# Six-layer cross network on one core: product 4 at two levels in both tiles, and more places for weights and blocks

## The chip, the cores and the metric

The kernel runs on one core of one Trainium2 chip. The time is device microseconds of the whole program, as the median of its runs. A profiled execution of its own gives the page and the trace.

## The reference

`x0` is [16384, 1024], `ws` is [6, 1024, 1024], `bs` is [6, 1024], all in bf16.

```python
x = x0
for l in range(6):
    proj = jnp.einsum('bd,de->be', x, ws[l]) + bs[l]
    x = x0 * proj + x
return x
```

Each layer is a product of the state x with a square matrix, a bias, an elementwise product with x0 and the addition of the state.

## The kernel before

**Tiles and units.** The 16384 rows are cut into 16 tiles ("pairs" in the code) of 1024 rows, and two tiles make a group that shares the weights of a layer. The work goes group by group, in it layer by layer, in it first tile ("lane 0"), second tile ("lane 1"). One tile in one layer is a *unit*: 96 units. Tiles lie transposed in SBUF, features on the partitions. Three x0 tiles (`x0T0` to `x0T2`, x0) and three state tiles (`xst0` to `xst2`, the running x) are used in turn, tile number modulo 3. So in each group one x0 tile and one state tile are idle between the previous group's output and the next group's input.

**Products.** A unit multiplies a 2 x 2 block matrix by a 2 x 2 block matrix (blocks of 512) with seven products in place of eight, in Winograd's form of Strassen's scheme. They are P1 to P7: VectorE (DVE) makes the sums of state blocks T1 to T4 (L432 to L435), TensorE (PE) multiplies, ScalarE (ACT) evicts PSUM into block tiles (Q, U, V, W, P1s, 5c, 3c; the trace calls them `ev`), and DVE adds these up and multiplies by x0. A product at one level (`group`, L313) is four PSUM banks with four matmuls of 512 columns each, so 16. Some products are done at a second level (`inner`, L491): seven smaller products, named such as 5p1 to 5p7, with four matmuls of 256 columns each, so 28, and more additions on DVE (t13, t2, t4 before, cc after) and more copies on ACT. The sums of weights that the scheme needs (5, 6, 7, 3 and, for the second level, 2i, 5i, 3i, 4i) are made in group 0 and written to DRAM (`Lc`), and the later groups load them.

**Which products are at two levels.** `inn` (L292): products 5, 2 and 3 in every tile but the first, which has 5 alone. Product 4 as well where `K4` (L152) lists the tile: in layer 0 in both tiles, in layers 1 to 4 in the second alone.

**What sets the order.** PE's order in a unit is written out by hand: `PE_FOUR` (L29) with four two-level products, `PE_TWO` (L25) with three, `PE_ONE5` (L21) for the first tile, `PE_FIRST` and `PE_LAST` at the ends. All other engines get theirs from `schedule` (L51), which plays the operations through with a cost for each and takes, on each engine, the ready one whose latest start is the earliest. So the order on DVE, ACT, POOL and SP is fixed when the program is built; on the chip each engine works through its queue in order, and waits.

**State.** After layer 0 the product with x0 becomes the state. In layers 1 to 4 the blocks listed in `DMA_RES` (L153: Q, U, V) are added into the state by an accumulating DMA that POOL issues (L564); W is added by DVE, except in group 0. Layer 5 adds all four on DVE. The block tiles change roles from unit to unit by `NEXT` (L176).

**Weights.** A ring of 12 places of 512 KB (`wp`); a layer has 11 weights. `ring_seq` (L219) gives the sequence and `pump` (L239) issues a load on SP as soon as the place 12 back has been read for the last time.

**Output and input.** At the end of a group the states are turned by DMA transposes on SP (L661) into an x0 tile and stored from there (L669): the first tile's in layer 5, the second's in layer 0 of the next group. The next group's x0 is loaded by DMA transposes from layer 4 on (`let`, `load`).

Of the kernel before, what the change touches and what calls it, by code (L numbers as in the profile page):

```python
# [9 lines left out]
ADD = mybir.AluOpType.add  # L10
# [9 lines left out]
""".split()  # L20
PE_ONE5 = """  # L21
P1.1 P1.0 P2.1 P6.0 P2.0 P1.2 5p5 5p1 P1.3 P6.1 5p2 P2.3 5p6 P6.2 P2.2 5p7 P6.3 5p3 P7.2 P7.3 5p4 P3.3 P7.1 P3.2 P7.0
P4.3 P4.2 P4.0 P3.1 P4.1 P3.0
""".split()
PE_TWO = """  # L25
5p5 P1.1 5p1 P1.0 P1.3 5p2 2p5 5p6 2p1 P1.2 5p3 2p2 5p7 2p6 P6.0 5p4 2p3 3p5 2p7 3p1 P6.1 2p4 3p2 3p6 P6.2 P6.3 3p3
3p7 P7.0 P7.1 P7.2 3p4 P7.3 P4.1 P4.0 P4.3 P4.2
""".split()
PE_FOUR = """  # L29
5p5 P1.0 5p1 2p5 2p1 P1.1 5p2 5p6 2p2 P1.2 2p6 P1.3 5p3 5p7 2p3 2p7 P6.0 3p5 5p4 2p4 P6.1 P6.3 3p1 4p5 P6.2 4p1 3p2  # L30
P7.0 4p2 3p6 4p6 P7.1 3p3 4p3 4p7 P7.2 3p7 4p4 P7.3 3p4
""".split()
PE_LAST = """
# [5 lines left out]

ACCUM = 9.0  # L40

# [84 lines left out]


@with_exitstack
def kernel(
# [19 lines left out]
    KQ, HQ, NQ = KH // 2, H // 2, NB // 2  # L149
    RING = 12  # L150
# [7 lines left out]
    wring = ctx.enter_context(tc.tile_pool(name="wring", bufs=RING))  # L158
    psum = ctx.enter_context(tc.tile_pool(name="ps", bufs=1, space=bass.MemoryType.PSUM))
# [13 lines left out]
    ip["4"] = ip["2"]  # L173
    P1s, P5s, Q, U, V, W, C3 = (work.tile([P, KH, KH, P], BF16, name=f"ev{i}") for i in range(7))
    EV = {"5c": P5s, "3c": C3, "U": U, "V": V, "W": W, "Q": Q, "P1s": P1s}
    NEXT = {"5c": "3c", "3c": "5c", "U": "W", "V": "U", "W": "V", "Q": "Q", "P1s": "P1s"}  # L176
    home = {r: r for r in EV}
    TURNED, rows = ((0, 0), (1, 0), (0, 1)), (P1s, U, V)
# [42 lines left out]
    for gl in range(NGROUP * L):  # L221
        if gl < L:
            ring_seq += [(gl, w, "load") for w in RAW] + [(gl, w, "make") for w in MADE]
        else:
            ring_seq += [(gl, w, "load") for w in "1 5 5i 2 2i 6 3 3i 7 4 4i".split()[:11 if gl % L in K4 else 10]]
    slot = {(gl, w): f"slot{i % RING}" for i, (gl, w, _) in enumerate(ring_seq)}
    wt, uses_left, live = {}, {}, []
    pos = {"next": 0}

    def ring_tile(key):  # L230
        while live and len(live) >= RING and uses_left.get(live[0], 0) == 0:
            live.pop(0)
        if len(live) >= RING:
            return None
        wt[key] = wring.tile([P, KH, H], BF16, name="wp")
        live.append(key)
        return wt[key]

    def pump():  # L239
        while pos["next"] < len(ring_seq):  # L240
            gl, w, kind = ring_seq[pos["next"]]
            if kind == "make":
                return
            t = ring_tile((gl, w))
            if t is None:
                return
            nc.sync.dma_start(t[:], w_src(gl % L, w))
            pos["next"] += 1

    def ring_make(gl, w):  # L250
        pump()
        assert ring_seq[pos["next"]] == (gl, w, "make"), (gl, w, ring_seq[pos["next"]])
        t = ring_tile((gl, w))
        assert t is not None, (gl, w, live, [uses_left.get(k) for k in live])
        pos["next"] += 1
# [22 lines left out]
    for u, (pr, l) in enumerate(units):  # L278
        one, first, last = plain(u), u == 0, u == NU - 1
        if not first:  # L280
            home = {r: home[NEXT[r]] for r in home}
        P1s, P5s, Q, U, V, W, C3 = (EV[home[r]] for r in ("P1s", "5c", "Q", "U", "V", "W", "3c"))
        CB = {"5": P5s, "2": Q, "3": C3, "4": W}
        gl, grp, lane = gl_of(u), pr // 2, pr % 2
        x0T, xst = x0Ts[pr % 3], xsts[pr % 3]
# [7 lines left out]
        ISW = [ISN[w] for w in ISLOT] + [f"is.{w}.{i}" for w in ISLOT for i in "5637"] if pr == 2 else []  # L293
        line = {w: i for i, w in enumerate(PE_FIRST if first else PE_LAST if last else PE_ONE5 if one else PE_FOUR if lane in K4.get(l, ()) and pr > 0 else PE_TWO)}

# [3 lines left out]
        def act(name, fn, rd, wr, biased_=False, u=u, occ=None):  # L299
            occ = occ or (0.571 if biased_ else 0.475)  # L300
            op(f"{name}@{u}", "ACT", occ, occ + 0.17, fn, rd, wr)
# [11 lines left out]
        def group(name, w, bank, bname, rhs, rname, m, start, gl=gl, kmajor=kmajor):  # L313
            def fn():
                for k in range(KH):
                    r = rhs[:, k, :] if kmajor else rhs[:, :, k, :]
                    o = bank[:] if kmajor else bank[:].rearrange("p (j r) -> p j r", r=P)
                    nc.tensor.matmul(o, lhsT=wt[(gl, w)][:, k, m * P:(m + 1) * P], rhs=r,  # L318
                                     start=(start and k == 0), stop=(k == KH - 1), skip_group_check=True)
# [24 lines left out]

        def let(q, sp, u=u, xst=xst):
            def fn():
                nc.gpsimd.dma_start(x0Ts[sp][0:1, q[1], q[0] * KH, :], xblk(xst, 1, 1)[0:1].rearrange("p j k r -> p (j k r)")[:, 0:NB])
            op(f"let@{u}", "POOL", 0.6, 2.5, fn, [XO[1, 1], XO[0, 1]], [f"x0.{sp}.{q[0]}{q[1]}"])

        def fence(q, sp, u=u):  # L350
            def fn():
                nc.gpsimd.dma_start(seen[:], x0Ts[sp][0:1, q[1], q[0] * KH, 0:32])
            op(f"fence@{u}", "POOL", 0.6, 0.6, fn, [f"x0.{sp}.{q[0]}{q[1]}"], ["xbar"])

        if l == 0 and lane == 1:
# [121 lines left out]
        if inn:  # L477
            for X, a, b in (("5", 0, 1), ("2", 2, 3), ("3", 0, 1), ("4", 2, 3))[:len(inn)]:
# [12 lines left out]
                def inner(i, bank, start, X=X, gl=gl, q=q, tk=tk, src=src, kmajor=kmajor):  # L491
# [5 lines left out]
                    def fn():  # L497
# [3 lines left out]
                        else:  # L501
                            wi = weight(gl, w) if gl < L else weight(gl, w)[:]
                            wv = wi.rearrange("p q (k e) -> p q k e", k=KQ)[:, {5: 0, 6: 1, 3: 2, 7: 3}[i]]
                        for m in range(KQ):
                            for k in range(KQ):
                                o = pX[bank][:, m * NQ:(m + 1) * NQ]
                                nc.tensor.matmul(o if kmajor else o.rearrange("p (j r) -> p j r", r=P), lhsT=wv[:, k, m * P:(m + 1) * P],  # L507
                                                 rhs=rhs(k), start=(start and m == 0 and k == 0), stop=(k == KQ - 1), skip_group_check=True)
                    if gl < L and w.endswith("i"):
# [38 lines left out]
        if not last:  # L548
            if not one:
                ttop("Q1", Q[:], Q[:], P1s[:], ADD, allm("Q") + allm("P1s"), allm("Q"))  # L550
            ttop("Ua", U[:], U[:], P5s[:], ADD, allm("U") + allm("5c"), allm("U"))
            if not one:
                ttop("Ub", U[:], U[:], C3[:], ADD, allm("U") + allm("3c"), allm("U"))
            if "4" in inn:
                ttop("Wa", W[:], W[:], V[:], ADD, allm("W") + allm("V"), allm("W"))
            ttop("Va", V[:], V[:], P5s[:], ADD, allm("V") + allm("5c"), allm("V"))
            for nm, C, q in (("Q", Q, (0, 0)), ("U", U, (0, 1)), ("V", V, (1, 1)), ("W", W, (1, 0))):
# [3 lines left out]
                ttop(nm + "m", C[:], C[:], x0j(*q), MULT, allm(nm) + [X0[q]], allm(nm))  # L561
                if nm in DMA_RES.get(l, "") or nm == "W" and grp == 0 and 0 < l < L - 1:
                    def acc(C=C, q=q, xst=xst):
                        nc.gpsimd.dma_start(xblk(xst, *q), C[:], accum_op=ADD)  # L564
                    op(f"{nm}x@{u}", "POOL", 1.0, ACCUM, acc, allm(nm) + [XO[q], "xbar"], [XO[q]])
                else:
                    ttop(nm + "x", xblk(xst, *q), C[:], xblk(xst, *q), ADD, allm(nm) + [XO[q]], [XO[q]])
        else:
# [7 lines left out]
            r0 = pr * PR  # L576
            END = NU * 22.95
            half = lambda s, h: [f"{s}.{2 * h}", f"{s}.{2 * h + 1}"]
# [57 lines left out]
        if grp == 0 and lane == 0:  # L636
            if first:
                op("gate@0", "POOL", 0.1, 0.3, lambda ga=ga, xst=xst: nc.gpsimd.tensor_copy(ga[:], xst[:, 0, 0, 0, 0, 0:1]), [XO[0, 0]], ["gate"])
            for w in MADE:
                save(w, lambda w=w, gl=gl: wt[(gl, w)][:], [f"w{gl}.{w}"], [w])  # L640
            for Xi in ISLOT:
# [32 lines left out]

    order, start, _ = schedule(ops)

    ctx.enter_context(tc.manual_schedule(
# [31 lines left out]

    held = [i for i in order if ops[i].name.startswith("ld") and ops[i].name.endswith(".1@1")]  # L710
    for i in held:
        ops[i].fn()
    for i in order:
        if i not in held:
# [35 lines left out]
```

## Time and profile before

| | us |
|---|---|
| median of 3 runs | 2217.83 |
| lowest and highest | 2217.66, 2217.92 |
| profiled execution | 2217.99 |
| its span | 2216.2 |

The granted clock is 1.00. In the page, lines such as `PE 2203.0 (99%)` give an engine's busy time, its share of the span and its instructions; PEld is PE's loading of weights into the array, which runs beside the matmuls. In the chain, a line is start, length, engine, tile and source line, and a piece `x20` is 20 instructions in a row. `ev`, `T`, `ti`, `ip`, `wp`, `xst`, `x0T` are tiles in SBUF, `pA` and `pX` are PSUM banks. `L318` is the matmul at one level, `L507` the one at two levels, `L337` and `L327` are evictions with and without bias, `L204` every DVE operation, `L564` the accumulating DMAs, `L247` the weight loads.

### The profile page before, as it was taken

Reading aid. Unit: us, or ns where it says so; the run is one execution under the profiler, and the core shown is the slowest. Engines: PE = TensorE matmul, PEld = TensorE weight load, DVE = VectorE, ACT = ScalarE, POOL = GpSimd, SP = SyncE. Lnnn points to the kernel's source line nnn. Section 1 sums busy time; section 2 is a strip of 40 time slices with the busy share of each in tenths; the row PEclk is TensorE's granted clock in tenths of the full one; section 3 lists DMA queues with packets and bytes.
Section 4 is the critical chain, followed back from the end, with each engine's and each line's share of the span. In section 5 each row is a group of like instructions: output and inputs, shape, how many; then the busy total and the mean of one; then the engine's idle time right before and its main releaser. Section 6 shows DMA issues by size and latency. Waiting matters only on the chain.

```text
span 2216.2 us, 39701 instructions
## 1 busy us (share of the span) xinstructions
PE 2203.0 (99%) x14637; PEld 1432.6 (65%) x14685; DVE 2143.7 (97%) x2539; ACT 2038.9 (92%) x3657; POOL 211.1 (10%) x271
## 2 busy tenths in 40 slices
PE   9999999999999999999999999999999999999998
PEld 5555666666666666666666666666666666666664
DVE  8999999999999999999999999999999999999997
ACT  7888899999999999999999999999999999999997
POOL 1132100110001100011000110011100111001110
PEclk9999999999999999999999999999999999999999
DMA  8788999768986689866898678976789777896777
GB/s 257 208 222 239 215 239 263 182 171 216 259 254 176 177 226 252 256 173 179 237 251 237 172 197 226 261 222 177 214 224 251 216 181 224 214 272 185 201 224 166
DMA packets 455460, 482.88 MB, mean 218 GB/s; under 512 B 269152, under 2 KB 381280, under 8 KB 455264
## 3 DMA queue, kind: packets, MB, share of 16 engines
q1 hardware_dynamic: 418352, 349.49, 53.5%
q0 software_dynamic: 36320, 130.57, 29.1%
q8 instruction: 115, 1.88, 0.3%
q14 instruction: 81, 0.66, 0.1%
q10 hardware_dynamic: 592, 0.27, 0.0%
HBM read 252.72 MB, written 58.20 MB: 140 GB/s over the span
## 4 chain that ended last, share of the span: by engine, by line
PE 99%; SPq 0%; DMA 0%; issue 0%; DVE 0%; DVEq 0%
PE pA L318 52%; PE pX L507 44%; PE pX L318 2%; DMA x0T<-in_x_dram 0%; SPq L691 0%; PE pA L611 0%; SPq L698 0%; DVE T L204 0%; SPq L704 0%; PE pX L611 0%; DVE xst L623 0%; SPq L701 0%; DVEq L204 0%
## 5 line engine op out<-in xcount | busy, mean ns | idle before, releaser
L507 PEld LDWEIGHTS <-wp 128*128 128x128 bf16 x8484 | 829.8, 98 | 275.4 <-issue 1.0
L337 ACT ACTIVATE ev<-pA,b_all 128x512 bf16<-128x512 f32 x1291 | 881.6, 692 | 107.5 <-PE pA L318 66.3
L318 PE MATMUL pA<-T,wp 128*128 128x512 bf16 x3825 | 922.2, 379 | 1.6
L318 PEld LDWEIGHTS <-wp 128*128 128x128 bf16 x5648 | 552.0, 98 | 478.4 <-issue 2.1
L327 ACT CAST ev<-pX 128x512 bf16<-128x512 f32 x1284 | 699.5, 595 | 24.2 <-PE pX L507 21.1
L507 PE MATMUL pX<-ti,wp 128*128 128x256 bf16 x4768 | 661.2, 273 | 0.0
L204 DVE TENSOR_TENSOR ev<-ev,ev 128x2048 bf16<-128x2048 bf16 x419 | 503.4, 1219 | 43.9 <-ACT ev L327 35.8
L204 DVE TENSOR_TENSOR ev<-ev,x0T 128x2048 bf16<-128x2048 bf16 (+1 forms) x324 | 386.0, 1210 | 2.3 <-ACT ev L337 1.2
L327 ACT COPY pX<-pX 128x512 f32<-128x512 f32 x638 | 370.8, 593 | 3.6
L318 PE MATMUL pA<-xst,wp 128*128 128x512 bf16 x1280 | 320.5, 379 | 0.0
L564 POOL DMA_DIRECT2D xst<-ev x200 | 172.3, 862 | 1296.8 <-ACT ev L337 445.6
L507 PE MATMUL pX<-xst,wp 128*128 128x256 bf16 x1736 | 260.5, 273 | 0.0
L507 PE MATMUL pX<-T,wp 128*128 128x256 bf16 x1628 | 244.3, 273 | 0.0
L204 DVE TENSOR_TENSOR ev<-ev,ip 128x1024 bf16<-128x1024 bf16 x319 | 214.4, 690 | 0.0
L204 DVE TENSOR_TENSOR T<-xst,T 128x2048 bf16<-128x2048 bf16 x160 | 195.6, 1223 | 1.0 <-PE pX L507 1.0
L204 DVE TENSOR_TENSOR T<-xst 128x2048 bf16<-128x2048 bf16 x160 | 195.6, 1223 | 0.0
L327 ACT CAST ip<-pX 128x512 bf16<-128x512 f32 x319 | 187.8, 589 | 2.1 <-PE pX L507 2.1
L204 DVE TENSOR_TENSOR xst<-ev,xst 128x2048 bf16<-128x2048 bf16 x116 | 141.8, 1224 | 0.1
L204 DVE TENSOR_TENSOR ti<-T,ti 128x512 bf16<-128x512 bf16 x282 | 119.6, 424 | 0.0
L204 DVE TENSOR_TENSOR ti<-xst 128x1024 bf16<-128x1024 bf16 x148 | 102.3, 691 | 9.3 <-PE pX L507 8.3
L204 DVE TENSOR_TENSOR ti<-xst,ti 128x1024 bf16<-128x1024 bf16 x148 | 101.8, 688 | 0.1
L204 DVE TENSOR_TENSOR ti<-T 128x1024 bf16<-128x1024 bf16 x141 | 97.3, 690 | 0.0
(57 smaller groups left out, 702.7 us busy)
## 6 DMA issues: line engine op xcount, KB each, us to landing
wp<-Lc SPq DMA_DIRECT2D x329, 512.0 KB, 6.1
xst<-ev POOLq DMA_DIRECT2D x200, 512.0 KB, 5.3
wp<-in_ws_dram SPq DMA_DIRECT2D x148, 512.0 KB, 6.7
out_dram<-x0T SPq DMA_DIRECT2D x60, 512.0 KB, 4.3
Lc<-wp POOLq DMA_DIRECT2D x24, 512.0 KB, 5.9
Lc<-xst POOLq DMA_DIRECT2D x23, 512.0 KB, 8.9
ev<-in_x_dram SPq DMA_DIRECT2D x3, 512.0 KB, 6.5
wp<-in_ws_dram SPq DMA_DIRECT2D x4, 256.0 KB, 7.4
```

The source lines that it names most:

```text
L204: nc.vector.tensor_tensor(out=o, in0=a, in1=b, op=op)
L318: nc.tensor.matmul(o, lhsT=wt[(gl, w)][:, k, m * P:(m + 1) * P], rhs=r, start=(start and k == 0), stop=(k == KH - 1), skip_group_check=True)
L327: act(name, lambda: nc.scalar.copy(out=dst, in_=src), rd, wr)
L337: act(name, lambda: nc.scalar.activation(out=dst, in_=src, func=IDENT, bias=b_all[:, c:c + 1], scale=1.0), rd, wr, True)
L507: nc.tensor.matmul(o if kmajor else o.rearrange("p (j r) -> p j r", r=P), lhsT=wv[:, k, m * P:(m + 1) * P], rhs=rhs(k), start=(start and m ...
L564: nc.gpsimd.dma_start(xblk(xst, *q), C[:], accum_op=ADD)
```

## The change

- Product 4 at two levels in both tiles of layers 1 to 4 (`K4`), and W by accumulating DMA as well in every group (`DMA_RES`).
- In layers 1 to 4 of the groups after the first, the idle x0 tile gives four more places for weights: 16 in all. Which weight goes to which place, and when it is issued, comes from a new function `plan_loads`, after `schedule` has run. A load gets a time before which it isn't issued: it is put behind the operations that the plan starts earlier, and waits for the newest matmul that then stands in PE's queue. Loads keep away from the bursts of accumulating DMAs where their need allows.
- In layers 1 to 5 the second tile's Q, U, V and W lie in the idle state tile.
- New orders for PE in `PE_ONE5` (now `PE_ONE_INNER`), `PE_TWO` and `PE_FOUR`, a new order of the loads, other turns of roles (`TURN`), other costs in the plan (biased eviction 0.571 to 0.583, copy 0.475 to 0.482, accumulate 9.0 to 9.5 in group 0 and 12 after), and Ua behind Ub and Wa.

```diff
 PE_TWO = """
+5p5 5p1 2p5 2p1 P1.1 5p6 5p2 P1.0 2p2 P1.2 5p7 5p3 P1.3 2p6 P6.0 3p5 5p4 2p3 P6.1 2p7 P7.0 3p1 2p4 P6.2 P6.3 P7.1 P7.2
+3p2 3p6 P7.3 P4.0 3p3 3p7 P4.2 P4.3 3p4 P4.1
 PE_FOUR = """
+5p5 5p1 2p5 P1.1 P1.3 5p2 2p1 5p6 P1.0 2p2 2p6 5p3 5p7 P1.2 2p3 2p7 5p4 P6.0 P6.3 2p4 3p5 3p1 P6.2 4p5 4p1 3p2 3p6
+P6.1 4p2 4p6 3p3 3p7 P7.0 P7.1 4p7 4p3 3p4 P7.3 P7.2 4p4
...
-ACCUM = 9.0
+ACCUM = (9.5, 12)
+RING = 12
+LOAD, BURST, LEAD, GRACE = 1.45, 2.9, 13, 4
+STORED, SPARE = 12.0, 14.0
+LOAD_ORDER = "5 2 1 2i 5i 6 3i 3 4i 4 7".split()
...
+def plan_loads(ops, start, ring_seq, layers):
...
+    for gl, w in loads:
+        grp, l = gl // layers, gl % layers
+        if l == 1 and (grp, 0) not in avail:
+            for q in range(4):
+                held[grp, q] = None
+                avail[grp, q] = named[f"sto{q // 2}{q % 2}.{2 * grp - 1}@{2 * layers * grp + 1}"] + STORED
+        able = [s for s in avail if not isinstance(s, tuple) or s[0] == grp and 0 < l < layers - 1]
...
+        s = min(spare or able, key=lambda s: (avail[s], str(s)))
...
+    for k, (free_at, _), due in zip(loads, ready, deadline):
+        while True:
+            t = max(t, min(free_at, bursts[b]))
+            if bursts[b] <= t and (free_at > t or bursts[b] + GRACE <= due):
+                t += BURST
...
-    K4 = {0: (0, 1), 1: (1,), 2: (1,), 3: (1,), 4: (1,)}
-    DMA_RES = {1: "QUV", 2: "QUV", 3: "QUV", 4: "QUV"}
+    K4 = {l: (0, 1) for l in range(L - 1)}
+    DMA_RES = {l: "QUVW" for l in range(1, L - 1)}
...
-            nc.sync.dma_start(t[:], w_src(gl % L, w))
+            ld = nc.sync.dma_start(t, w_src(gl % L, w))
+            if (gl, w) in held:
+                tc.add_manual_dep(ld.ins, newest["pe"].ins.name, mybir.DependencyInfo(mybir.DependencyClass.Sync, mybir.DependencyReason.DATA))
...
+        idle = (2 * grp + 2) % 3
+        home = dict(cycle)
+        if grp > 0 and lane and 0 < l and not last:
+            home.update({r: "S" + r for r in "QUVW"})
+        EV.update({"S" + r: xsts[idle][:, i // 2, i % 2] for i, r in enumerate("QUVW")})
...
-                if nm in DMA_RES.get(l, "") or nm == "W" and grp == 0 and 0 < l < L - 1:
+                if nm in DMA_RES.get(l, ""):
...
-        pump()
+        pump(start[i])
```

More of the change, by code (lines that the diff above doesn't have):

```diff
@@ L125, in schedule @@
     return order, start, late
+def plan_loads(ops, start, ring_seq, layers):
+    first, free, named = {}, {}, {}
+    for i, o in enumerate(ops):
+        named[o.name] = start[i]
+        for k in o.weights:
+            first[k] = min(first.get(k, 1e9), start[i])
+            free[k] = max(free.get(k, 0.0), start[i] + o.occ)
+    made = [(gl, w) for gl, w, _ in ring_seq if gl < layers]
+    held = {n % RING: k for n, k in enumerate(made)}
+    avail = {s: free[k] for s, k in held.items()}
+    loads = [(gl, w) for gl, w, _ in ring_seq if gl >= layers]
+    where, before, ready = {}, {}, []
+    for gl, w in loads:
[5 more added lines that the diff above has]
+        able = [s for s in avail if not isinstance(s, tuple) or s[0] == grp and 0 < l < layers - 1]
+        spare = [s for s in able if isinstance(s, tuple) and l == layers - 2 and avail[s] < first[gl, w] - SPARE]
+        s = min(spare or able, key=lambda s: (avail[s], str(s)))
+        where[gl, w], before[gl, w] = s, held[s]
+        ready.append((avail[s], first[gl, w]))
+        held[s], avail[s] = (gl, w), free[gl, w]
+    deadline, nxt = [0.0] * len(loads), 1e9
+    for n in range(len(loads) - 1, -1, -1):
+        nxt = min(nxt, ready[n][1] - LEAD)
+        deadline[n] = nxt
+        nxt -= 1.3 * LOAD
+    issue, t, b = {}, 0.0, 0
+    bursts = sorted([start[i] + 1.0 for i, o in enumerate(ops) if o.eng == "POOL" and o.name[1:3] == "x@"]) + [1e9]
+    for k, (free_at, _), due in zip(loads, ready, deadline):
[3 more added lines that the diff above has]
+                t += BURST
+                b += 1
+            else:
+                break
+        issue[k] = t
+        t += LOAD
+    return where, before, issue, {k: first[k] for k in loads}
 @with_exitstack
@@ L174 @@
     P1s, P5s, Q, U, V, W, C3 = (work.tile([P, KH, KH, P], BF16, name=f"ev{i}") for i in range(7))
+    ring = [work.tile([P, KH, H], BF16, name=f"wp{i}") for i in range(RING)]
     EV = {"5c": P5s, "3c": C3, "U": U, "V": V, "W": W, "Q": Q, "P1s": P1s}
-    NEXT = {"5c": "3c", "3c": "5c", "U": "W", "V": "U", "W": "V", "Q": "Q", "P1s": "P1s"}
-    home = {r: r for r in EV}
+    cycle = {r: r for r in EV}
+    home = cycle
     TURNED, rows = ((0, 0), (1, 0), (0, 1)), (P1s, U, V)
@@ L224, with pump @@
         else:
-            ring_seq += [(gl, w, "load") for w in "1 5 5i 2 2i 6 3 3i 7 4 4i".split()[:11 if gl % L in K4 else 10]]
-    slot = {(gl, w): f"slot{i % RING}" for i, (gl, w, _) in enumerate(ring_seq)}
-    wt, uses_left, live = {}, {}, []
+            ring_seq += [(gl, w, "load") for w in LOAD_ORDER if w != "4i" or gl % L in K4]
+    made = [(gl, w) for gl, w, _ in ring_seq if gl < L]
+    where = {k: i % RING for i, k in enumerate(made)}
+    before = {k: made[i - RING] if i >= RING else None for i, k in enumerate(made)}
+    slot = {k: f"slot{i}" for k, i in where.items()}
+    wt, uses_left = {}, {}
     pos = {"next": 0}
     def ring_tile(key):
-        while live and len(live) >= RING and uses_left.get(live[0], 0) == 0:
-            live.pop(0)
-        if len(live) >= RING:
-            return None
-        wt[key] = wring.tile([P, KH, H], BF16, name="wp")
-        live.append(key)
+        if uses_left.get(before[key], 0) > 0:
+            return None
+        i = where[key]
+        if isinstance(i, tuple):
+            wt[key] = x0Ts[(2 * i[0] + 2) % 3][:, i[1] % 2, i[1] // 2 * KH:(i[1] // 2 + 1) * KH, :]
+        else:
+            wt[key] = ring[i][:]
         return wt[key]
-    def pump():
+    held, newest = {}, {}
+    def pump(time=0.0):
         while pos["next"] < len(ring_seq):
             gl, w, kind = ring_seq[pos["next"]]
-            if kind == "make":
+            if kind == "make" or held.get((gl, w), 0.0) > time:
                 return
@@ L253, in ring_make @@
         t = ring_tile((gl, w))
-        assert t is not None, (gl, w, live, [uses_left.get(k) for k in live])
+        assert t is not None, (gl, w)
         pos["next"] += 1
@@ L280 @@
         if not first:
-            home = {r: home[NEXT[r]] for r in home}
+            turn = TURN[0 if pr < 2 else 1 + pr % 2]
+            cycle = {r: cycle[turn[r]] for r in cycle}
+        gl, grp, lane = gl_of(u), pr // 2, pr % 2
+        idle = (2 * grp + 2) % 3
[3 more added lines that the diff above has]
+        EV.update({"S" + r: xsts[idle][:, i // 2, i % 2] for i, r in enumerate("QUVW")})
         P1s, P5s, Q, U, V, W, C3 = (EV[home[r]] for r in ("P1s", "5c", "Q", "U", "V", "W", "3c"))
         CB = {"5": P5s, "2": Q, "3": C3, "4": W}
-        gl, grp, lane = gl_of(u), pr // 2, pr % 2
         x0T, xst = x0Ts[pr % 3], xsts[pr % 3]
@@ L293 @@
         ISW = [ISN[w] for w in ISLOT] + [f"is.{w}.{i}" for w in ISLOT for i in "5637"] if pr == 2 else []
-        line = {w: i for i, w in enumerate(PE_FIRST if first else PE_LAST if last else PE_ONE5 if one else PE_FOUR if lane in K4.get(l, ()) and pr > 0 else PE_TWO)}
+        line = {w: i for i, w in enumerate(PE_FIRST if first else PE_LAST if last else PE_ONE_INNER if one else PE_FOUR if lane in K4.get(l, ()) and pr > 0 else PE_TWO)}
         def pe(name, occ, fn, rd, wr, weights=(), u=u, gl=gl, line=line, at=0.0):
@@ L317, in fn @@
                     o = bank[:] if kmajor else bank[:].rearrange("p (j r) -> p j r", r=P)
-                    nc.tensor.matmul(o, lhsT=wt[(gl, w)][:, k, m * P:(m + 1) * P], rhs=r,
-                                     start=(start and k == 0), stop=(k == KH - 1), skip_group_check=True)
+                    newest["pe"] = nc.tensor.matmul(o, lhsT=wt[(gl, w)][:, k, m * P:(m + 1) * P], rhs=r,
+                                                    start=(start and k == 0), stop=(k == KH - 1), skip_group_check=True)
             if first and name in ("P5.0", "P5.1"):
@@ L343, in load, with let @@
             op(f"ld{q[0]}{q[1]}.{pt}@{u}", "SP", 2.7, 6.0, fn, [], [f"x0.{pt % 3}.{q[0]}{q[1]}"], at=at, after=after)
-        def let(q, sp, u=u, xst=xst):
+        def let(q, sp, u=u, xst=xst, grp=grp):
             def fn():
+                assert all(uses_left.get(k, 0) == 0 for k, i in where.items() if i in [(grp, n) for n in range(4)])
                 nc.gpsimd.dma_start(x0Ts[sp][0:1, q[1], q[0] * KH, :], xblk(xst, 1, 1)[0:1].rearrange("p j k r -> p (j k r)")[:, 0:NB])
@@ L353, in fence @@
             op(f"fence@{u}", "POOL", 0.6, 0.6, fn, [f"x0.{sp}.{q[0]}{q[1]}"], ["xbar"])
+        if lane == 0 and (grp > 0 and l == 1 or grp > 1 and l == 0 or grp == NGROUP - 1 and l == L - 1):
+            state = pr % 3 if l == 0 else idle
+            op(f"lend@{u}", "POOL", 0.0, 0.0, lambda: None, (), [f"S{r}.{m}" for r in "QUVW" for m in range(KH)] + [f"xs.{state}.{a}{b}" for a, b in QD])
         if l == 0 and lane == 1:
@@ L501, in fn @@
                         else:
-                            wi = weight(gl, w) if gl < L else weight(gl, w)[:]
+                            wi = weight(gl, w) if gl < L else weight(gl, w)
                             wv = wi.rearrange("p q (k e) -> p q k e", k=KQ)[:, {5: 0, 6: 1, 3: 2, 7: 3}[i]]
@@ L506, in fn @@
                                 o = pX[bank][:, m * NQ:(m + 1) * NQ]
-                                nc.tensor.matmul(o if kmajor else o.rearrange("p (j r) -> p j r", r=P), lhsT=wv[:, k, m * P:(m + 1) * P],
-                                                 rhs=rhs(k), start=(start and m == 0 and k == 0), stop=(k == KQ - 1), skip_group_check=True)
+                                newest["pe"] = nc.tensor.matmul(
+                                    o if kmajor else o.rearrange("p (j r) -> p j r", r=P), lhsT=wv[:, k, m * P:(m + 1) * P],
+                                    rhs=rhs(k), start=(start and m == 0 and k == 0), stop=(k == KQ - 1), skip_group_check=True)
                     if gl < L and w.endswith("i"):
@@ L561 @@
                 ttop(nm + "m", C[:], C[:], x0j(*q), MULT, allm(nm) + [X0[q]], allm(nm))
-                if nm in DMA_RES.get(l, "") or nm == "W" and grp == 0 and 0 < l < L - 1:
+                if nm in DMA_RES.get(l, ""):
                     def acc(C=C, q=q, xst=xst):
                         nc.gpsimd.dma_start(xblk(xst, *q), C[:], accum_op=ADD)
-                    op(f"{nm}x@{u}", "POOL", 1.0, ACCUM, acc, allm(nm) + [XO[q], "xbar"], [XO[q]])
+                    op(f"{nm}x@{u}", "POOL", 1.0, ACCUM[grp > 0], acc, allm(nm) + [XO[q], "xbar"], [XO[q]])
                 else:
@@ L576 @@
             r0 = pr * PR
[L577 removed]
+            END = NU * 22.8
             half = lambda s, h: [f"{s}.{2 * h}", f"{s}.{2 * h + 1}"]
@@ L675 @@
     order, start, _ = schedule(ops)
+    places, olds, issue, _ = plan_loads(ops, start, ring_seq, L)
+    where.update(places)
+    before.update(olds)
+    held.update(issue)
     ctx.enter_context(tc.manual_schedule(
@@ L708 @@
     nc.sync.dma_start_transpose(out=blk(x0Ts[0], 1, 1), in_=x0[NB:2 * NB, H:2 * H])
-    held = [i for i in order if ops[i].name.startswith("ld") and ops[i].name.endswith(".1@1")]
-    for i in held:
+    early = [i for i in order if ops[i].name.startswith("ld") and ops[i].name.endswith(".1@1")]
+    for i in early:
         ops[i].fn()
     for i in order:
-        if i not in held:
+        if i not in early:
             ops[i].fn()
```

20 lines of the change are left out of this document (8 added, 12 removed), and 3 rows, old and new, of the table TURN.

## The prediction, made before the result was known

> **What bounds the kernel now.** I read the profile page first: busy shares, then the chain that ended last.
>
> ```profile
> span 2216.2 us, 39701 instructions
> PE 2203.0 (99%) x14637; PEld 1432.6 (65%) x14685; DVE 2143.7 (97%) x2539; ACT 2038.9 (92%) x3657; POOL 211.1 (10%) x271
> ...
> PE 99%; SPq 0%; DMA 0%; issue 0%; DVE 0%; DVEq 0%
> ```
>
> The chain is matrix work from end to end: the time is the sum of the matmuls as long as nothing makes TensorE (PE) wait. But VectorE (DVE) stands at 97%, so the second question is how much DVE room the change uses up.
>
> Next, the chain in order of time inside one group, for the real price of a matmul:
>
> ```profile
> 445.77 4.32 PE pA L318 x20
> ...
> 457.04 1.75 PE pX L507 x16
> ...
> 491.34 4.32 PE pA L318 x20
> ...
> 536.91 4.32 PE pA L318 x20
> ...
> 559.90 4.32 PE pA L318 x20
> ```
>
> A matmul over 512 columns takes 4.32 / 20 = 0.216 us of the chain, one over 256 columns 1.75 / 16 = 0.109 us. The x20 piece is the tail of a PE_TWO unit. It returns every 45.57 us in layers 1 to 4 (a PE_TWO and a PE_FOUR unit) and after 559.90 - 536.91 = 22.99 us in layer 5 (two PE_TWO units). So PE_TWO takes 22.99 us and PE_FOUR 45.57 - 22.99 = 22.58.
>
> Then the busy times by stage: layers 1, 2, 3, 4, 5 of a group and layer 0 of the next (columns: PE, weight loads, DVE, ACT, POOL, clock, DMA share, GB/s).
>
> ```profile
> 605.20:650.80 45.60, 45.55 (x309) 30.16 (x309) 45.57 (x55) 42.91 (x77) 3.98 (x5) 1.00 0.90 242
> 650.80:696.40 45.60, 45.60 (x311) 30.13 (x310) 44.01 (x52) 42.75 (x78) 5.14 (x6) 1.00 0.73 200
> 696.40:742.00 45.60, 45.60 (x311) 30.16 (x309) 43.89 (x52) 42.75 (x78) 5.15 (x6) 1.00 0.74 198
> 742.00:787.50 45.50, 45.50 (x310) 30.07 (x308) 43.80 (x52) 42.66 (x77) 5.16 (x6) 1.00 0.73 196
> 787.50:833.50 46.00, 46.00 (x309) 30.04 (x308) 44.43 (x51) 42.70 (x77) 2.25 (x3) 1.00 0.84 208
> 833.50:878.80 45.30, 45.04 (x305) 30.22 (x309) 45.30 (x55) 42.76 (x78) 0.00 (x0) 1.00 1.02 262
> ```
>
> Two things are to be seen. DVE is busy without a gap in layers 0 and 1, and PE loses next to nothing there: a full DVE need not cost PE time. And DVE is busy 267.0 of the 273.6 us of a group, 6.6 idle. Who stops it, and how the transfers stand, is in the waits and in the issues:
>
> ```profile
> DVE ev L204 <- ACT ev L327: 35.8, 28, 1.9
> DVE ti L204 <- PE pX L507: 8.3, 28, 0.5
> ```
>
> Both happen 28 times, as often as there are layers 1 to 4 in seven groups: 44 / 28 = 1.6 us a layer, where DVE has caught up.
>
> **The change part by part.** The instructions of both built kernels, counted by kind, give what is removed and added.
>
> *PE.* 448 matmuls of 512 columns go and 784 of 256 come: in each of 28 units (first tile, layers 1 to 4, seven groups) 16 against 28. 16 x 0.2159 - 28 x 0.1091 = 3.454 - 3.053 = 0.40 us a unit, 11.2 us in all (the two unit lengths give 22.99 - 22.58 = 0.41, 11.5 in all). All of it is on the chain. Weight loads rise by 336 (98 ns each in the groups); in PE_FOUR units now they lie beside the matmuls, so nothing more for them.
>
> The mean durations in the groups would mislead here: 273 ns for 256 columns, 379 for 512, so 28 x 0.273 - 16 x 0.379 = 1.58 us more a unit, 44 us more in all. The chain's 0.109 and 0.216 speak against that reading, since 20 matmuls fit into 4.32 us. The Trainium skill, "TensorE: Matmul & The Clock Gate", section "Back-to-back issue gap", holds a rule that speaks against the change: in a sustained stream 512 columns cost about 131 ns and 128 columns 81, so that halving the width does not halve the cost. By an estimate midway on that line (98 ns for 256 columns) the unit would lose 0.64 us and the sum would be 18 us slower; the 216 ns of the trace contradicts its 131, and the chain decides.
>
> *DVE.* Start to start in the timeline, an operation on 2048 elements takes 1.135 us, on 1024 0.60, on 512 0.335. A new two-level product 4 adds one t13 and one cc (1024), t2 and t4 (512) and Wa (2048): 1.135 + 2 x 0.60 + 2 x 0.335 = 3.0 us. Against that the addition of W into the state leaves DVE in both tiles: -2 x 1.135 = -2.27. Net +0.74 us a layer, +20.6 in all. A group then has 267.0 + 4 x 0.74 = 269.9 us of DVE work in 273.6 - 1.6 = 272.0 us of PE work: 2.1 us of room are left of 6.6. I cost this at nothing, because DVE's stops come where it has caught up and has nothing ready; without that cover every microsecond of its standing over 2.1 in a group would be one on PE.
>
> *ACT.* Per unit 4 biased evictions go and 7 copies come. Layer 0 already runs two PE_FOUR units and shows ACT at 42.76 of 45.30, as in layers 1 to 4. Nothing.
>
> *POOL and accumulating DMAs.* 56 more W transfers, 0.86 us of POOL each: 48 us on an engine that is 10% busy; only the accumulates behind it wait. Their use of the DMA engines: six take a share of 0.384 in layer 2, so two more add 0.128: layers 2 to 4 go from 0.73 to 0.86, layer 1 from 0.90 to about 1.0, as full as layer 0 is now. An accumulate lands in 5.3 us (median), 6.5 in layer 1, 11.7 at worst. The tightest in the new order is U: its last input is 3p4, 2.6 us before the end of the unit; eviction 0.6, cc 0.6, three DVE steps 3.4, POOL 0.9, landing 6.5, then T1 and 5t13 1.7: 13.7 us, and the tile's next unit starts 2.6 + 22.6 = 25.2 us after 3p4. 11 us are left for queueing. W has more, since 4p5 comes 13 us into its unit.
>
> *Weights and SP.* The same 477 loads are issued, in a new order, 84 of them to the idle x0 tile, each held back by a wait on a PE instruction. SP's queue is in order, so behind a waiting load stand further loads, the transposes of the output and the stores. From the built order and the matmul prices I took the PE work between the instruction that releases a load and the first matmul that reads it: before at least 12.6 us, after at least 10.9 (once per group, a load released 10.9 us before layer 1 begins to use it; two more kinds at 11.3 and 12.2), all others over 12.5. Loads land in 6.3 us at the median, 7.0 to 7.4 in layer 1, 13.2 at worst. At the median nothing; at the worst value 13.2 - 10.9 = 2.3 us, in seven groups 16.
>
> *Idle state tile, exchanged blocks, PE_ONE_INNER, the place of Ua.* The same operations on other addresses. The block of the second tile in the idle state tile must wait for the output transposes of that tile, issued in layer 0, a whole unit (22.6 us) before the first eviction; they land in 5.9. In group 0, where DVE is as full and PE solid too, the new order could win or lose a tenth or two. Nothing.
>
> *Instruction fetch.* In each layer 0, at a DMA share of about 1.0, PE waits once on "issue" for 0.17 us, which no other layer shows. If layer 1 becomes as full: 0 to 7 x 0.17 = 1.2 us. I take half, 0.6, as its share would come just to that point.
>
> **Sum.** The profiled execution took 2217.99 us (span 2216.2 and 1.8 around it): 2217.99 - 11.2 + 0.6 = 2207.4; the median of the runs lies 0.16 under it, so 2207.2.
>
> **The rivals.**
> 1. *Loads come late.* Layer 1 with its full DMA engines delays loads with 10.9 us of margin. For it: 13.2 us has occurred. Against: the full layer 0 lands loads in 4.9 us at the median, and no PE wait on a load stands in the steady layers. All seven groups at the worst: 2207.2 + 16 = 2223; more likely two or three of them, 2210 to 2217.
> 2. *DVE becomes the bound* (the slower side). If DVE still stops for 1.6 us a layer, 6.6 a group, in an order with 2.1 of room, PE loses 4.5 a group: 7 x 4.5 = 32, 2239. At half of these stops (3.3) it loses 1.2 a group: 2215.6. It gets slower than before from 2.1 + 1.6 = 3.7 us of stops a group. For it: each stop is on an eviction or a matmul, and these stay. Against: in layers 0 and 1 the stops vanish as soon as DVE has work in hand. The Trainium skill, "SBUF — State Buffer", section "Who interferes with whom", says that an operation with two SBUF inputs contends with a GpSimd instruction that reads SBUF; more POOL issues would then slow DVE. A POOL issue from 681.43 to 682.29 shows no such thing: the DVE operations around it start at 681.76, 682.89 and 684.03, the usual 1.13 apart.
> 3. *A matmul of half the width costs more than half*, as the durations in the groups would have it: 2217.8 + 44 = 2262. The chain all but excludes it.
>
> That the change does not do what it says is excluded by the counts.
>
> **Chances.** Forecast 0.64 (2205 to 2209.5: no fetch waits and the larger unit difference below, two or three tenths of a microsecond in each of seven groups above). Rival 1: 0.14, most of it under 2217. Rival 2: 0.21, of which 0.07 is the half case (2209.5 to 2217) and 0.14 slower than before. Rival 3: 0.01. The range 2205 to 2217 takes in the forecast, 0.10 of rival 1 and the half case: about 0.8. A measurement of this kernel can tell about 0.2% (4.4 us) from no change: faster (under 2213.4) 0.76, same 0.08, slower 0.16.
>
> **What would show it.** PE still at 99% and the chain all PE; a layer pair of 45.17 us instead of 45.57; DVE at about 98%, its waits on ACT and PE down from 44 us to 15 or less; accumulates landing in 5 to 8 us. It is wrong if PE shows waits on DVE (rival 2) or weight loads on a DMA (rival 1) of more than a microsecond a group.

## The result, and the profile after

The changed kernel takes 2275.8 us (median of 6 runs, 2271.0 to 2278.4) against 2217.6 in the same session: 1.026 times as long, interval 1.0246 to 1.0273. It is slower, by 58 us; the forecast was 2207.2, so 68.6 us have to be explained.

The page of the changed kernel, its busy times and the shares of the chain:

```profile
PE 2211.2 (97%) x14973; PEld 1471.8 (65%) x15021; DVE 2171.1 (95%) x2623; ACT 2068.1 (91%) x3741; POOL 259.5 (11%) x327
...
PE 92%; DMA 3%; DVE 2%; ACT 1%; issue 1%; SPq 1%; POOLq 0%; ACTq 0%; DVEq 0%
```

PE is down from 99% to 97%, and a DMA has come into the chain. Next the stretches of the trace after: two stretches of a layer's length inside a group (from late in layer 1 into layer 3), and 4.5 us at the change from one group to the next (columns as in the prediction).

```profile
651.00:696.17 45.17, 45.17 (x323) 31.31 (x321) 44.75 (x55) 43.72 (x82) 6.84 (x8) 1.00 0.97 246
696.17:741.34 45.17, 45.17 (x321) 31.16 (x319) 44.79 (x55) 43.34 (x81) 6.88 (x8) 1.00 0.89 222
577.50:582.00 4.50, 4.44 (x23) 2.90 (x23) 4.50 (x6) 3.45 (x8) 0.00 (x0) 0.62 0.23 95
```

Inside a group PE is solid, and the same matmuls come back in the next layer after 45.2 us; 45.17 were forecast. The loss sits where groups meet: from the second group on, one group starts 281.0 to 283.2 us after the other, instead of some 272. The change from the first group to the second shows only a stop of 1.2 us. The waits of the trace after (who waits for whom: sum, times, longest) name three engines there, with nearly the same sum:

```profile
DVE ti L256 <- DMA x0T<-in_x_dram: 40.8, 12, 4.4
PE pX L578 <- ACT pX L393: 40.5, 14, 6.8
ACT ev L393 <- DVE xst L256: 39.1, 6, 7.2
```

Read from below they are one stop: PE waits for a copy on ACT, ACT for DVE, DVE for the next group's x0. PE has six such stops of 5.2 to 6.8 us. The chain of the trace after, in order of time, runs through it once:

```profile
563.66 8.07 DMA x0T<-in_x_dram
...
571.82 0.69 DVE ti L256
572.51 1.13 DVE T L256
...
576.91 0.60 ACT pX L393
...
577.56 3.52 PE pX L578 x16
```

The last transpose of the first tile's x0 lands at 571.73; PE comes back at 577.56, after a stop of 6.7 us, and its first 16 matmuls of 256 columns then take 3.52 us instead of 1.75. Why is the transpose so late? The queue of SP, first before, then after (start, length, what was issued):

```profile
537.38 8.43 SPq L342 DMA_TRANSPOSE x0T<-in_x_dram  x4
547.33 0.34 SPq L247 DMA_DIRECT2D wp<-Lc  x1
547.72 3.31 SPq L342 DMA_TRANSPOSE x0T<-in_x_dram  x1
```

```profile
535.49 11.43 SPq L408 DMA_TRANSPOSE x0T<-in_x_dram  x3
549.46 0.39 SPq L305 DMA_DIRECT2D wp<-in_ws_dram  x1
549.94 2.90 SPq L408 DMA_TRANSPOSE x0T<-in_x_dram  x1
...
563.66 7.38 SPq L408 DMA_TRANSPOSE x0T<-in_x_dram  x2
```

Which transpose belongs to which tile is read from the built order on SP. Before, the run of four from 537.38 to 545.8 is one of the second tile and three of the next group's first tile; the first tile's fourth goes out at 547.72, behind one weight load. After, three of the *second* tile go first, and two of these wait in the queue for DVE. Then SP stands until 549.46 in front of a weight load that waits for PE, and the four of the first tile follow one by one between weight loads, at 549.94, 553.51, 558.04 and 563.66. `let`, the POOL transfer behind which they may go, was issued at 537.24 (before: 532.63) and lands in 2.8 us at the median. So they were ready some 10 us before the first of them went out. `let` itself is not late on the chip: it is issued 27.6 us before the next group's first matmul, against 27.3 before.

### The profile page after: what moved, and what is told of

Same layout as the page of the kernel before. It is cut to its first block, busy times and chain, and to the rows that moved or that the text cites. A ratio compares the mean times of both kernels' runs of the same rounds, so it can differ in the third digit from the quotient of the medians.

```text
span 2276.3 us, 40609 instructions
## 1 busy us (share of the span) xinstructions
PE 2211.2 (97%) x14973; PEld 1471.8 (65%) x15021; DVE 2171.1 (95%) x2623; ACT 2068.1 (91%) x3741; POOL 259.5 (11%) x327
## 4 chain that ended last, share of the span: by engine, by line
PE 92%; DMA 3%; DVE 2%; ACT 1%; issue 1%; SPq 1%; POOLq 0%; ACTq 0%; DVEq 0%
PE pX L578 45%; PE pA L384 45%; PE pX L384 2%; DMA x0T<-in_x_dram 2%; DVE T L256 1%; DVE ev L256 1%; DVE xst L256 0%; ACT pX L393 0%; DVE ti L256 0%; ACT ev L403 0%; ACT ev L393 0%; DMA xst<-x0T 0%; SPq L767 0%; ACT ip L393 0%; SPq L408 0%
## 5 line engine op out<-in xcount | busy, mean ns | idle before, releaser
L578 PEld LDWEIGHTS <-wp 128*128 128x128 bf16 x7644 | 753.0, 99 | 279.3 <-issue 55.7
L384 PEld LDWEIGHTS <-wp 128*128 128x128 bf16 x4304 | 421.8, 98 | 377.6 <-issue 4.5
L384 PE MATMUL pA<-T,wp 128*128 128x512 bf16 x2705 | 650.2, 379 | 1.6
L403 ACT ACTIVATE ev<-pA,b_all 128x512 bf16<-128x512 f32 x883 | 607.3, 696 | 39.4 <-PE pA L384 22.8
L256 DVE TENSOR_TENSOR ev<-ev,ev 128x2048 bf16<-128x2048 bf16 (+1 forms) x283 | 341.3, 1208 | 9.5 <-ACT ev L403 7.0
L256 DVE TENSOR_TENSOR ev<-ev,x0T 128x2048 bf16<-128x2048 bf16 (+2 forms) x188 | 223.7, 1192 | 1.1 <-ACT ev L403 0.8
L403 ACT ACTIVATE xst<-pA,b_all 128x512 bf16<-128x512 f32 x296 | 202.3, 693 | 9.9 <-PE pA L384 5.3
L578 PEld LDWEIGHTS <-x0T 128*128 128x128 bf16 x1624 | 158.8, 98 | 40.3 <-issue 2.3
L256 DVE TENSOR_TENSOR xst<-xst,ev 128x2048 bf16<-128x2048 bf16 x136 | 165.6, 1218 | 3.6 <-ACT ev L393 1.2
L256 DVE TENSOR_TENSOR xst<-xst,x0T 128x2048 bf16<-128x2048 bf16 x136 | 164.3, 1216 | 0.2
L384 PE MATMUL pA<-T,x0T 128*128 128x512 bf16 x672 | 163.3, 379 | 0.0
```

Of the source, the lines that this page charges most:

```text
L256: nc.vector.tensor_tensor(out=o, in0=a, in1=b, op=op)
L384: newest["pe"] = nc.tensor.matmul(o, lhsT=wt[(gl, w)][:, k, m * P:(m + 1) * P], rhs=r, start=(start and k == 0), stop=(k == KH - 1), skip_ ...
L403: act(name, lambda: nc.scalar.activation(out=dst, in_=src, func=IDENT, bias=b_all[:, c:c + 1], scale=1.0), rd, wr, True)
L578: newest["pe"] = nc.tensor.matmul(o if kmajor else o.rearrange("p (j r) -> p j r", r=P), lhsT=wv[:, k, m * P:(m + 1) * P], rhs=rhs(k), sta ...
```

## The experiments

**Theories.** A: the order on SP makes the loss. The plan fixes it, and the plan now costs an accumulate at 12 us instead of 9, so `let`, which waits for the last accumulates, stands late in the plan, and the first tile's transposes are put behind others and behind weight loads. After the first four runs it was sharpened (A2): what blocks SP is the weight load that is held back, and `let`'s late place in the plan is what puts the transposes behind it. B, the rival: the transposes are slow in themselves, because the added accumulates fill the DMA engines; their place in the queue matters little. C, a second rival: the accumulates, and `let` with them, end later. For each run stands below the text on record, then the times (before, in these sessions, 2217.5 to 2217.8; after 2275.8).

**e1_own_first**: in the changed kernel, the second tile's x0 loads go behind the first tile's in the plan.

```diff
-                load(pr, q, ARRIVE["next"] if u == 1 else 0.0)
+                load(pr, q, ARRIVE["next"] if u == 1 else 0.0, after=[f"ld{a}{b}.{pr - 1}@{u - 4}" for a, b in QD] if grp else ())
```

> The changed kernel, with one edit: the four x0 loads of the next group's second tile are put behind the four of its first tile on SP (in the changed kernel three of them stand ahead). Theory A (the order on SP makes the first tile's x0 late: in the trace its loads go out at 549.9 to 563.7 though the transfer that lets them go was issued at 537.2): the stop of PE at each group boundary, 6.7 us and the low clock after it, goes, and 2206 to 2215 us are left. Rival B (the transposes are slow because the DMA engines are full): the order matters little, 2250 or more. Rival C (the accumulates before the loads end later, 10 us later against the end of the unit than before): half comes back, 2235 to 2245.

2280.6 us, 1.028 (1.0265 to 1.0295): no gain. SP of this kernel shows why:

```profile
538.08 1.93 SPq L408 DMA_TRANSPOSE x0T<-in_x_dram  x1
548.69 0.39 SPq L305 DMA_DIRECT2D wp<-in_ws_dram  x1
549.99 0.34 SPq L305 DMA_DIRECT2D wp<-Lc  x1
550.38 4.40 SPq L408 DMA_TRANSPOSE x0T<-in_x_dram  x1
```

The second tile's loads were not all that the first tile's stood behind. With them gone, SP stands from 540.0 in front of the held weight load at 548.69, which is still ahead of all but one. The expectation had the wrong obstacle.

**e2_accum_9**: in the changed kernel, the old cost of an accumulate in the plan, after group 0.

```diff
-ACCUM = (9.5, 12)
+ACCUM = (9.5, 9.0)
```

> The changed kernel with the plan's cost of an accumulating DMA in the groups after the first put back from 12 to 9.0 us; no instruction is added or removed, but the plan puts two of the second tile's x0 loads ahead of the first tile's in place of three. Theory A: one load less ahead is worth some 3.6 us of SP time a boundary, or up to 5 with the weight load between: 2276 less 25 to 40, so 2236 to 2251. Rival B: no difference, 2270 or more. Rival C: no difference, 2265 or more.

2237.3 us, 1.009 (1.0075 to 1.0105). One number that exists only in the plan gives back 38 of the 58 us; not one instruction is added or taken away. Four transposes now go out before the held load (from 536.26), two of them the first tile's.

**e4_products_alone**: the kernel before, with the two-level product 4 in both tiles and W by DMA, and nothing else of the change.

```diff
-    K4 = {0: (0, 1), 1: (1,), 2: (1,), 3: (1,), 4: (1,)}
-    DMA_RES = {1: "QUV", 2: "QUV", 3: "QUV", 4: "QUV"}
+    K4 = {l: (0, 1) for l in range(L - 1)}
+    DMA_RES = {l: "QUVW" for l in range(1, L - 1)}
```

> The kernel before, with two lines changed: product 4 at two levels in both tiles of layers 1 to 4, and W added by accumulating DMA in all groups. The places for weights (12), the block tiles, PE's orders and the order of the x0 loads on SP (one load of the second tile ahead) stay as before. Theory A: PE's 11.2 us show, as no load is late: 2204 to 2214. Rival B: more accumulates slow the transposes here too, 2240 or more. Rival C: the accumulates end later here too, 2225 to 2245. If DVE is the bound (room 2.1 us a group): 2215 to 2239, with PE waits on DVE spread over the layers.

2360.9 us, 1.064 (1.0628 to 1.066). Of the expectations only the open one of B (2240 or more) holds the number, and its mechanism is not what the trace shows: PE's long stops lie in layers 1 to 4, and from the first to the last matmul on x0 layer 0 takes as long as before. Its waits hold a line that neither full kernel shows:

```profile
ACT ev L327 <- DMA xst<-ev: 54.3, 27, 2.5
```

Evictions stand and wait until an accumulate has read the block tile that they are to overwrite; DVE waits about as long (54.5 us) for accumulates to land. This suggests that W by DMA needs the other homes for the blocks, or the other order, that the change gives it. How much the new places, orders and turns of roles each contribute was not tried.

**e3_one_tile**: the changed kernel, product 4 at two levels in the second tile alone again.

```diff
-    K4 = {l: (0, 1) for l in range(L - 1)}
+    K4 = {0: (0, 1), 1: (1,), 2: (1,), 3: (1,), 4: (1,)}
```

> The changed kernel with product 4 at two levels in the second tile alone in layers 1 to 4, as before; W by accumulating DMA, 16 places, the idle state tile, the new orders and costs stay. The plan puts two of the second tile's x0 loads ahead. Theory A: the stop of PE at the boundaries is there without the new products: 2236 to 2251 as with the other kernel with two loads ahead, plus 11 of PE, 2247 to 2262. If the new products are what costs the time: 2218 to 2225.

2262.5 us, 1.020 (1.0181 to 1.0215), 0.5 us over what A allowed. Without the products the kernel stays 45 us slower than before: the loss does not hang on them. But the order differs too, so their price cannot be read from this.

**e6_right_after_let**: the changed kernel; `let` and the four transposes of the next group's first tile are issued as soon as the four accumulates of the second tile in layer 4 have been. The plan and all instructions are the same, only their place in POOL's and SP's queues is not.

```diff
+    now = {}
+    for n, o in enumerate(ops):
+        if o.name.startswith("let@"):
+            v = int(o.name[4:])
+            now[frozenset(named[f"{r}x@{v}"] for r in "QUVW")] = [n] + [j for j in range(n + 1, n + 5)]
+    early += [j for js in now.values() for j in js]
+    done = set()
     for i in order:
...
+        done.add(i)
+        for k in [k for k in now if k <= done]:
+            for j in now.pop(k):
+                ops[j].fn()
```

> The changed kernel, with the same plan and the same instructions, but the transfer that lets the next group's x0 in and the four x0 loads of its first tile are issued as soon as the four accumulates of layer 4 are, so that on SP they stand ahead of the second tile's three loads and, above all, ahead of the weight loads that are held back for a matmul. Theory A2 (what was wrong in theory A is which instruction blocks SP: in the traces of the changed kernel and of own-loads-first a held weight load goes out at 549.5 and 548.7, and the first tile's loads behind it): the loads run from 538 to 547, the stop at the boundary goes, 2206 to 2216. Now the weight loads stand behind seven transposes; if these come late in turn, 2216 to 2235. Rival B (full DMA engines make the transposes slow): 2260 or more.

2217.6 us, 0.9999 (0.999 to 1.0008): 58.2 us are back by a change of place alone. The number lies 1.6 us above A2's range and in the one given for weight loads that come late in turn; but PEld waits for such loads for 1.0 us in the whole run, and e12 below finds 5.3 us at the end of the program. SP of this kernel, and the line of its PE waits that stood at 40.5 us after:

```profile
536.00 17.29 SPq L408 DMA_TRANSPOSE x0T<-in_x_dram  x7
553.38 0.95 SPq L305 DMA_DIRECT2D wp<-in_ws_dram  x1
```

```profile
PE pX L578 <- ACT pX L393: 1.7, 6, 0.3
```

Seven transposes run without a weight load between them. B falls: the accumulates and the bytes are those of the changed kernel, and PE does not stop. C falls too: `let` is again issued 27.6 us before the next group's first matmul, so only the place on SP has moved. From the profile after to this one, PE's waits on ACT and DVE fall from 44.3 to 1.7 us and its busy time from 2211.2 to 2197.5: 42.6 us of standing and at least 13.7 of slow matmuls (48 records of matmuls are missing in the profile after), 56.3 of the 61.3 by which the spans differ.

**e8_right_after_let_spread**: e6 with the line of e1.

> As right-after-let, and the plan also lets the second tile's x0 loads follow the first tile's, so that they are spread between the weight loads. Theory A2: the stop goes, and the weight loads wait behind four transposes only: 2205 to 2212. Rival B: 2260 or more. If DVE bounds what is left: 2212 to 2230 with PE waits on DVE.

2245.2 us, 1.012 (1.0101 to 1.0137), a miss. The first tile's four transposes go out at once, but the second tile's move back in the plan, and the same fault turns up at the second tile. SP of this kernel, its last two:

```profile
569.14 6.16 SPq L408 DMA_TRANSPOSE x0T<-in_x_dram  x2
```

PE then stops for 2.7 us at 578.26, still in the first tile's unit of layer 0: DVE stands for the second tile's x0 (3.0 us before 572.11, 1.2 before 575.45) with work for the first tile behind it in its queue.

**b1_before_let_late**: the kernel *before*, with a `let` that lands 10 us later in the plan. The number is the time that `schedule` plays through; no instruction is added or taken away.

```diff
-            op(f"let@{u}", "POOL", 0.6, 2.5, fn, [XO[1, 1], XO[0, 1]], [f"x0.{sp}.{q[0]}{q[1]}"])
+            op(f"let@{u}", "POOL", 0.6, 12.5, fn, [XO[1, 1], XO[0, 1]], [f"x0.{sp}.{q[0]}{q[1]}"])
```

> The kernel before, with one number of its plan changed: the transfer that lets the next x0 in is taken to land 10 us later than it does (2.5 to 12.5 us). The same instructions on every engine; on SP the second to fourth x0 load of the first tile now stand behind five weight loads that wait for PE. Theory A2: the kernel before gets the stops at the group boundaries as well, by the same blocking: 2225 to 2280. Rival (the new placements or the accumulates of W are needed for the stops): no difference, 2217 to 2220.

2274.4 us, 1.026 (1.0242 to 1.027). The kernel before can be given the whole loss without any part of the change: 57 us. Its SP looks like that of the changed kernel:

```profile
540.75 1.90 SPq L342 DMA_TRANSPOSE x0T<-in_x_dram  x1
550.69 0.34 SPq L247 DMA_DIRECT2D wp<-Lc  x1
551.13 5.05 SPq L342 DMA_TRANSPOSE x0T<-in_x_dram  x2
```

There is no `plan_loads` here. An ordinary weight load, which waits until its place in the ring has been read, holds up the transposes as well as a planned one.

**e11_one_tile_after_let**: e6 with the edit of e3, so that the price of the products can be read in a sound order.

> Right-after-let, with product 4 at two levels in the second tile alone in layers 1 to 4. It asks what the products are worth once the x0 loads are not late. If the price from the chain holds (0.40 us a unit, 28 units), PE_TWO units come back and 11 us more than right-after-let: 2227 to 2231. If DVE bounded right-after-let (its room was 2.1 us a group) the lighter DVE would give something back: 2216 to 2224.

2229.6 us, 1.0054 (1.0042 to 1.0067). The two-level product 4 in the first tile is worth 2229.6 - 2217.6 = 12.0 us; the prediction had 11.2. This kernel has the products of the kernel before and takes 11.9 us more than it: so much the rest of the change costs even with the x0 loads in place, and the next run finds part of it.

**e12_after_let_tail**: e6 still takes 36.0 us from the start of the 32 matmuls in a row on pX in the last unit to the end of the span, the kernel before 30.1. Tile 14's last blocks are finished late on DVE, so its last two stores go out at 2197.63 and 2201.16. Here these stores get a due time in the plan.

```diff
-                op(f"sto{q[0]}{q[1]}.{pt}@{u}", "SP", 0.5, 8.0, sto, [sname], ())
+                op(f"sto{q[0]}{q[1]}.{pt}@{u}", "SP", 0.5, 8.0, sto, [sname], (), due=NU * 22.8 - 12 if pt == NPAIR - 2 else FAR)
```

> Right-after-let, and in the plan the stores of the last tile but one (transposed on SP ahead of the last tile's own transposes) get a due time, 12 us before the plan's end, so that DVE finishes the blocks that they wait for earlier. No instruction is added. In right-after-let the last of these stores is issued 22.2 us after PE starts the last 32 matmuls of products 5 and 6 on pX, against 16.9 in the kernel before, and from there to the end it takes 36.0 us against 30.1. If late output transposes make the tail longer, 4 to 6 us go: 2211 to 2214. If not: 2216 to 2219.

2212.3 us, 0.9976 (0.9967 to 0.9985). The end takes 30.5 us and the last stores go out at 2188.04 and 2193.12: 5.3 us were lost at the end of the program. The diff also lowers `END`, the due time of the last tile's output in the plan, from 22.95 to 22.8 us a unit, which the description of the change does not name. In the order that the code builds, the old number puts the last additions of tile 14's U and W on DVE ahead of the last tile's `Qa`, where the kernel before has them, and changes little else; no run tells its share of the 5.3 us.

**e13_after_let_tail_accum_9**: e12 with the edit of e2.

> After-let-tail, with the plan's cost of an accumulating DMA at 9.0 us. With the x0 loads right behind what lets them in, the cost no longer decides their place: the same as after-let-tail within 3 us, 2209 to 2216. If the cost had also an effect of its own (DVE's order, the place of the other loads), more than 3 us from it.

2209.4 us, 0.9962 (0.995 to 0.9975), the best of all: 8.3 us under the kernel before. The page of this kernel:

```profile
PE 2197.5 (100%) x15021; PEld 1466.7 (66%) x15021; DVE 2166.5 (98%) x2623; ACT 2060.9 (93%) x3741; POOL 259.5 (12%) x327
```

With the loads in place, the plan's cost of an accumulate is worth 2.9 us more; a group takes 272.21 us instead of 272.65.

## Why the prediction was wrong

The 68.6 us between forecast and result fall into four parts, each but the last the difference of two runs: 58.2 the place of `let` and the first tile's transposes on SP (after to e6), 5.3 the end of the program (e6 to e12), 2.9 what else the plan's cost of an accumulate moves (e12 to e13), 2.2 not assigned.

- **The step that failed is "Weights and SP".** It names what stands behind a waiting load on SP ("further loads, the transposes of the output and the stores") and then prices only the weight loads, by their margin to PE. The transposes of the *next x0* stand in that queue too, and for them no margin was taken. In the profile before they had some: three of the first tile's four were issued by 545.8 and the fourth at 547.72, and DVE does not wait for one of them. In the new order, which could be read before any run, all four come behind a held load, which on the chip went out at 549.46, and the fourth goes out at 563.66.
- **The plan's costs were priced at nothing.** The new cost of 12 for an accumulate stands in the diff; by the trace before it lands in 5.3 us. Since `schedule` sets the order on four engines by these numbers, the cost is an edit like any other. That it works through the plan is shown from both sides: e2 takes it back and gains 38 us, b1 puts a late `let` into the kernel before and loses 57.
- **The end of the program was not priced.** Nothing in the sum looks past the last group, where DVE's order decides when the output can go: 5.3 us.
- **The 0.6 us for instruction fetch** have no run behind them. The wait of 0.17 us in layer 0 before is one of PEld, not of PE; in layer 1 of e6 (607.6 to 652.8), at a DMA share of about 1.06, PEld has no wait on "issue" at all. That it is a fetch is shown nowhere.
- **PE was right.** 11.2 us forecast, 12.0 measured (e11 to e6), and a layer pair of 45.2 us (forecast 45.17). Rival 3 is out: half the width costs half.
- **DVE was right where the loads come in time.** Forecast 269.9 of 272.0 us in a group; after, DVE is busy 44.75 to 44.79 us in a stretch of 45.17, and PE does not stop there; a group of e13 (562.9 to 835.1) holds 270.2 us of DVE work. Rival 2 had the right sign of the total and the wrong mechanism: DVE does stand before PE at the seams, but because its own queue waits for x0, and that goes with e6 though DVE has the same work.
- **ACT, POOL and the DMA engines** cost nothing in the steady layers, as forecast. Cut at the layers (665.0, 710.2, 755.5, 800.9), the DMA share after is 0.92, 0.82 and 0.95 in layers 2 to 4 of a group, where 0.86 was estimated for each, and 1.05 in layer 1, where it was about 1.0; an accumulate lands in 6.7 us at the median and 10.4 at worst (5 to 8 forecast), and no margin was used up.
- **Rival 1 was wrong.** PE waits 1.0 us or less in a whole run for a weight load to land. The margins of 10.9 us were enough; the loads did their harm by standing in the queue, not by being late.
- **The tests named in the prediction** said: wrong if PE waits on DVE or on loads. PE's wait is written against ACT instead; only the line by line way back (ACT behind DVE, DVE behind the transpose) gives the cause.

Still open are the 2.2 us, and what the new places and orders are worth one by one.

## What to carry to other kernels

For every engine whose queue is in order, list what stands *behind* each instruction that can wait, and take a margin for each kind of it, not only for the kind that the change is about; a DMA that starts the next stage belongs on that list first. Where a plan fixes the order, a changed cost in it is a changed order, and is compared in the built order before any price is worked out. A loss that shows as one stop per outer loop is looked for where the loops meet, and is traced backwards over engines, since the wait names only the last of them.

## What the runs showed of the hardware

A stop of PE costs more than its length. After the 6.7 us at the seam, the granted clock is 0.62 over the next 4.5 us, and the first 16 matmuls of 256 columns take 3.52 us instead of 1.75. The Trainium skill, "TensorE: Matmul & The Clock Gate", section "Part 1: The HAM clock gate (the "warmup" mystery)", says that TensorE falls to half its clock after an idle window of about 3.4 us and returns after as long a busy one. The six long stops of the trace after fit this: the clock is 0.50 for 3.3 to 6.0 us after each of them, 30.7 us together. By an estimate from these, half of that time, some 15 us, comes on top of the stops; PE's busy time differs by at least 13.7. But here shorter stops were enough as well. In e8 the clock is 0.50 from 581.21 to 584.62 after a stop of 2.7 us, and in e1 from 590.84 to 594.25 after one of 2.0 us, while a stop of 2.1 us (after, at 1692.93) did not lower it.

One DMA transpose takes SP longer between weight loads: 8.43 us for four in a row before, 2.1 each, but 2.9 to 5.6 where they alternate with weight loads (2.90 and 3.38 after, 4.40 and 5.61 in e1). So a transpose pushed in between loads is late twice: it starts late, and it holds up the queue for longer. Which of the other transfers makes it longer, no run separates.
